# Weight conversion on VectorE in five pieces, and an opening in another order, in a spectral mixer with an MLP

## The chip, the cores and the metric

One NeuronCore of a Trainium2 chip runs the whole kernel in one launch. The metric is device microseconds of one execution; lower is better.

## The reference

For each of 8 batches, x (3072 positions, 256 channels) goes through a real FFT over the positions, a complex 256x256 product with bias, soft shrinkage and the inverse FFT; the result feeds an MLP with a softplus.

```python
X = np.fft.rfft(x, axis=1)                       # x: 8 x 3072 x 256
Yr = Xr @ w_r - Xi @ w_i + b_r
Yi = Xr @ w_i + Xi @ w_r + b_i
Y = sign(Y) * max(abs(Y) - 0.01, 0)              # Yr and Yi apart
y = np.fft.irfft(Y, n=3072, axis=1)              # then 24576 x 256
h = y @ w_in                                     # 256 x 2048
g = np.maximum(h, 0) + np.log1p(np.exp(-np.abs(h)))
out = g @ w_out                                  # 2048 x 256
```

## The kernel before, in words

Both FFTs are matmuls with constant tables. One batch passes through the stages `s1` (16 products of 96x512, the first DFT factor), `s3` (the second factor, for 12 groups `gp`), `mix` (complex weights and bias; the shrinkage `cl`, `shrunk`, `sh`, `sl` follows), `s4` (first inverse factor) and `s5` (second inverse factor). Between s1 and s3 (`a_dr`, from batch 1 on) and between s4 and s5 (`d_dr`) the data go through DRAM. The MLP takes y in products that save a multiplication by Strassen-like sums: its first layer writes `psc` and `pse`, VectorE adds (`t`, L542), ScalarE makes the softplus, `gh` and VectorE `gl` (L558), the high and low halves of the second layer's operand `pso`. Each fp32 product is three fp32r products of a high and a low half (L213 to L215).

The MLP's weights arrive as float64 words and are turned on the chip into a high and a low half, eight times `w1` (7 tiles of 128x128 with the Strassen sums, 896 KB with both halves) and eight times `w2` (512 KB). `load_w` brings the words, `split_w` converts: VectorE makes the exponent and mantissa by bit operations (L158 to L164), GpSimd multiplies and adds (L171, L180 to L184), VectorE makes the four sums (L188 to L191), ScalarE copies the high half (L192), VectorE subtracts (L196) and `store` writes the tile to DRAM (L99). The converted tile is tagged `wp` and there is one buffer for it (`bufs=1`). `stream_w` (L209) later loads a converted weight for every key of four MLP steps.

The order is written out by a table of steps (L674 to L760): 72 steps −72 to −1 in front, which take batch 0 through all stages and batch 1 through s1 (the first key's y comes from four `s5` at −4 to −1), then 768 MLP steps, four per key. In each step the program issues the MLP's products, one product of the other stages (`steps`), the loads that `fill` has for it, and what an earlier step has put into the queue `later`. Ten conversions begin in front, one every fourth step from −46; six begin at MLP steps 1, 5, 9, 13, 17 and 21. SyncE's queue (SP) carries nearly every DMA in program order; a wait of one holds the ones behind it. DMAs signal on eight hardware lanes in turn (DMAHW0 to 7). While `early` holds (up to step −2), tiles come from other tags and s1's odd columns are copied from PSUM by VectorE (L265).

Of the kernel before, what the change touches and what calls it, by code (L numbers as in the profile page):

```python
# [17 lines left out]
P = 128  # L18
# [15 lines left out]
def tile_spectral_mixer_mlp(ctx, tc, x, w_r, w_i, bias, bias_0, w_in, w_out, f, f_hi, f_lo, g1, g3, g3_hi, g3_lo, hm, out):  # L34
# [101 lines left out]
    def load_w(which, m2):  # L136

        if early:
            st = sb.tile([P, 1024 + 4 * N1], F32, tag="dp", name="w64", bufs=4)[:, :1024]
        else:  # L140
            st = sb.tile([P, 1024], F32, tag="w64", name="w64", bufs=1)
        nc.sync.dma_start(st.rearrange("p (a n) -> p a n", a=2).bitcast(U32), (w_in if which else w_out)[:, m2])
        stages[which, m2] = st

    def split_w(which, m2):

        st = stages.pop((which, m2)).bitcast(U32).rearrange("p (n w) -> p n w", w=2)
# [12 lines left out]
        v.tensor_scalar(out=ui, in0=ti, scalar1=0xFF800000, scalar2=None, op0=ALU.bitwise_and)  # L164

        def second():
            nc.scalar.mul(lw.bitcast(F32), lw, 2.0 ** -52)
            later.append(third)

        def third():  # L170
            g.tensor_tensor(out=u, in0=lw.bitcast(F32), in1=u, op=ALU.mult)  # L171
            n = 7 * P if which else 2 * D
            w = sb.tile([P, 2 * 7 * P], F32R, tag="wp", name="wp", bufs=1)[:, :2 * n]
            hi, lo, src = w[:, :n], w[:, n:], w[:, n:].bitcast(F32)
            if which:

                tm, um = [a.rearrange("p (k m n) -> p m k n", k=2, m=2) for a in (t, u)]
                a21 = tm[:, 1, 0]
                o = [src[:, i * P:(i + 1) * P] for i in range(7)]
                g.tensor_tensor(out=src[:, A11 * P:(A11 + 2) * P].rearrange("p (k n) -> p k n", k=2), in0=tm[:, 0], in1=um[:, 0], op=ALU.add)  # L180
                g.tensor_tensor(out=a21, in0=a21, in1=um[:, 1, 0], op=ALU.add)
                g.tensor_tensor(out=o[A22], in0=tm[:, 1, 1], in1=um[:, 1, 1], op=ALU.add)
            else:
                g.tensor_tensor(out=src, in0=t, in1=u, op=ALU.add)  # L184

            def high():
                if which:
                    v.tensor_tensor(out=o[S1], in0=a21, in1=o[A22], op=ALU.add)  # L188
                    v.tensor_tensor(out=o[S3], in0=o[A11], in1=a21, op=ALU.subtract)
                    v.tensor_tensor(out=o[S2], in0=o[S1], in1=o[A11], op=ALU.subtract)  # L190
                    v.tensor_tensor(out=o[S4], in0=o[A12], in1=o[S2], op=ALU.subtract)  # L191
                nc.scalar.copy(hi, src)  # L192
                later.append(low)

            def low():
                v.tensor_tensor(out=lo, in0=src, in1=hi.bitcast(F32), op=ALU.subtract)  # L196
                store((w1_dr if which else w2_dr)[m2][:, :], w.bitcast(F32), ("w", which, m2))

            later.append(high)

        later.append(second)
# [46 lines left out]
    def s1(b, c):  # L248
# [141 lines left out]
    def mix_sums(b, gp, lh, ll, real):  # L390
# [20 lines left out]
        v.tensor_scalar(out=cl, in0=z, scalar1=-LAM, scalar2=LAM, op0=ALU.max, op1=ALU.min)  # L411

        t = sb.tile([P, 512], F32, tag="v", name="shrunk", bufs=1)
        for c in range(2):
            for g in range(2):
                src = slice(g * 64, g * 64 + 64), slice(c * D, c * D + D)
                dst = slice(c * 64, c * 64 + 64), slice(g * D, g * D + D)
                v.tensor_tensor(out=t[dst], in0=z[src], in1=cl[src], op=ALU.subtract)
# [213 lines left out]
    with tc.manual_schedule():  # L632
# [71 lines left out]
        for t, i, j in ((t0 + 15, 0, 4), (t0 + 16, 4, 12), (t0 + 22, 12, NG)):  # L704
            at(t, nc.sync.dma_start, g1_0[:, i:j], g1[:, i:j])
        at(t0 + 18, nc.sync.dma_start, bias0, bias_0)
        at(-6, nc.sync.dma_start, bias_sb, bias)
        for k in range(2):
            at(t0 + 14 + k, load_mix, k)
            at(t0 + 18 + k, split_mix, k)  # L710
        for j in range(NM):
            t = t0 + 26 + 4 * j if j < 10 else 1 + 4 * (j - 10)
            at(t - (6 if j < 10 else 2), load_w, (j + 1) % 2, j // 2)
            before[t] = (j + 1) % 2, j // 2
        for c in need_d(0):
            at(first.index(("s4", 0, NP - 1)) + t0 + 4, load_d, 0, 0, c)
        for i, (t, src) in enumerate(((fh, f_hi), (fl, f_lo), (g3h, g3_hi), (g3l, g3_lo))):
            at(4 * i - 9, nc.gpsimd.dma_start, t, src)
        at(-1, early.clear)
        for k in range(2):  # L720
            at(-1, load_mix, k)
            at(1 + 2 * k, combine_mix, 1 + k)

        nt = NT
        for b in range(B):
            for bp in range(1, NPAIR):
                plan_s5(b, bp, nt * b + 2 * NM * bp - 14)
            if b + 1 < B:
                plan_mix(b + 1, *((5, 4.9) if b == 0 else (nt * b - 4, 5.6)))
                plan_s5(b + 1, 0, nt * (b + 1) - 14)  # L730
        for b in range(2, B):
            plan_s1(b, *((14, 4.6) if b == 2 else (nt * (b - 2) - 4, 5.4)))
        keys = [(b, bp, mp) for b in range(B) for bp in range(NPAIR) for mp in range(NM // 2)]
        for i, key in enumerate(keys):
# [3 lines left out]
            else:  # L738
                at(-3, stream_w, 1, 0, key)
                at(-2, stream_w, 0, 0, key)  # L740
        keys.append(None)
        for i in range(min([*fill, *steps]), nt * B + 3):
            due = len(later)
            other = split_w(*before.pop(i)) if i in before else iter(())
            if i >= 0:
                g, s = divmod(i, 4)
# [11 lines left out]
            for _ in other:  # L758
                pass
# [101 lines left out]
```

## Time and profile before

| | us |
|---|---|
| median of three runs (2713.51 to 2718.43) | 2714.6 |
| the profiled execution | 2714.95 |
| its span, first to last instruction | 2713.2 |
| TensorE (PE) busy | 2614.4 (96%) |
| VectorE (DVE) busy | 1624.9 (60%) |
| ScalarE (ACT) busy | 1708.0 (63%) |
| GpSimd (POOL) busy | 302.0 (11%) |

All rows are from the one profiled execution. The shares are means over a span that is mostly the steady MLP; the steps in front and the first MLP steps have to be read in stretches of their own. In a row of waits, "a <- b" is an engine that stood idle before instruction a until b ended. SPq is the queue of SyncE's DMAs.

### The profile page before, as it was taken

The numbers are of one execution on the slowest core, as the hardware profiler recorded it, in microseconds if no ns is written. First come the engines' busy times: TensorE is split into PE (matmuls) and PEld (weight loads), VectorE is DVE, ScalarE is ACT, GpSimd is POOL, SyncE is SP. The second block draws the span as 40 slices with busy tenths as digits, with TensorE's granted clock in tenths as the row PEclk, the third lists the DMA queues.
The fourth block names the chain that finished last, engine by engine and source line by source line (L and its number), as shares of the span: only waits on it lengthen the run. The fifth ranks groups of instructions, "written<-read, shape, count | busy, mean of one in ns | idle before, by whom it ended". The sixth has DMA issues, their size and how long they took to land.

```text
span 2713.2 us, 36252 instructions
## 1 busy us (share of the span) xinstructions
PE 2614.4 (96%) x13053; PEld 2190.6 (81%) x13053; DVE 1624.9 (60%) x2701; ACT 1708.0 (63%) x3093; POOL 302.0 (11%) x302
## 2 busy tenths in 40 slices
PE   7658999999999999999999999999999999999999
PEld 5437888888888888888878888788887888888887
DVE  3647665567656666466664666556664666644554
ACT  2336666666666666666666666666666666666665
POOL 1422110100101101011011010110010000000000
PEclk8869999999999999999999999999999999999999
DMA  5656556565565564555645655556555455455543
GB/s 195 206 191 222 181 167 199 172 197 166 167 197 171 185 189 143 192 183 177 202 145 174 205 176 161 186 164 198 174 173 177 162 169 188 142 160 176 176 154 111
DMA packets 186115, 479.73 MB, mean 177 GB/s; under 512 B 18096, under 2 KB 86960, under 8 KB 185936
## 3 DMA queue, kind: packets, MB, share of 16 engines
q1 hardware_dynamic: 185376, 476.95, 54.9%
q8 instruction: 103, 1.69, 0.3%
q0 software_dynamic: 560, 0.47, 0.1%
q14 instruction: 76, 0.62, 0.1%
HBM read 390.31 MB, written 83.89 MB: 175 GB/s over the span
## 4 chain that ended last, share of the span: by engine, by line
PE 87%; DMA 5%; DVE 4%; ACT 2%; POOL 1%; issue 1%; SPq 0%; DVEq 0%; ACTq 0%; POOLq 0%
PE pso L213 12%; PE pso L214 12%; PE pso L215 12%; PE psc L213 6%; PE psc L215 6%; PE psc L214 6%; PE pse L213 5%; PE pse L215 5%; PE pse L214 5%; PE psf L460 4%; PE psf L214 4%; PE psf L215 4%; PE psf L213 4%; PE psf L292 2%; DMA a_dr<-a 2%
## 5 line engine op out<-in xcount | busy, mean ns | idle before, releaser
L558 DVE TENSOR_TENSOR gl<-t,gh 128x512 fp32r<-128x512 f32 x768 | 532.3, 693 | 367.0 <-ACT gh L552 363.7
L542 DVE TENSOR_TENSOR t<-pse,t 128x512 f32<-128x512 f32 x576 | 396.2, 688 | 441.5 <-ACT t L537 285.1
L537 ACT COPY t<-psc 128x512 f32<-128x512 f32 x576 | 336.9, 585 | 492.3 <-PE psc L215 490.4
L213 PE MATMUL pso<-gh,w 128*128 128x512 f32 x1536 | 616.5, 401 | 0.0
L214 PE MATMUL pso<-gl,w 128*128 128x512 f32 x1536 | 600.6, 391 | 0.0
L215 PE MATMUL pso<-gh,w 128*128 128x512 f32 x1536 | 600.2, 391 | 0.0
L552 ACT CAST gh<-t 128x512 fp32r<-128x512 f32 x768 | 476.8, 621 | 61.8 <-PE pso L215 38.1
L548 ACT ACTIVATE t<-t 128x512 f32<-128x512 f32 x576 | 364.4, 633 | 68.7 <-DVE t L542 67.9
L215 PEld LDWEIGHTS pso<-gh,w 128*128 128x128 f32 x1536 | 289.1, 188 | 62.5
L213 PE MATMUL psc<-y_sb,w 128*128 128x512 f32 x768 | 302.8, 394 | 34.8 <-ACT t L537 16.8
L213 PEld LDWEIGHTS pso<-gh,w 128*128 128x128 f32 x1536 | 290.2, 189 | 54.7
L214 PEld LDWEIGHTS pso<-gl,w 128*128 128x128 f32 x1536 | 290.2, 189 | 51.4
L215 PE MATMUL psc<-y_sb,w 128*128 128x512 f32 x768 | 300.5, 391 | 0.0
L214 PE MATMUL psc<-y_sb,w 128*128 128x512 f32 x768 | 300.1, 391 | 0.0
L213 PE MATMUL pse<-y_sb,w 128*128 128x512 f32 x576 | 228.2, 396 | 14.7 <-DVE t L542 14.6
L114 POOL TENSOR_TENSOR xl<-xt,xh 96x512 fp32r<-96x512 f32 x96 | 124.5, 1300 | 960.7 <-ACT xh L105 823.7
L215 PE MATMUL pse<-y_sb,w 128*128 128x512 f32 x576 | 225.4, 391 | 0.0
L214 PE MATMUL pse<-y_sb,w 128*128 128x512 f32 x576 | 225.3, 391 | 0.0
L494 POOL TENSOR_TENSOR y_sb<-raw,y_sb 128x512 fp32r<-128x512 f32 x72 | 95.8, 1331 | 1130.8 <-ACT y_sb L491 1130.8
L213 PEld LDWEIGHTS psc<-y_sb,w 128*128 128x128 f32 x768 | 144.8, 189 | 72.3 <-ACT t L537 22.3
L215 PEld LDWEIGHTS psc<-y_sb,w 128*128 128x128 f32 x768 | 144.9, 189 | 31.1
L214 PEld LDWEIGHTS psc<-y_sb,w 128*128 128x128 f32 x768 | 144.9, 189 | 29.6
(123 smaller groups left out, 3640.8 us busy)
## 6 DMA issues: line engine op xcount, KB each, us to landing
w<-w_dr SPq DMA_DIRECT2D x192, 896.0 KB
w<-w_dr SPq DMA_DIRECT2D x192, 512.0 KB
dp<-d_dr SPq DMA_DIRECT2D x80, 384.0 KB
xt<-in_x SPq DMA_DIRECT2D x128, 192.0 KB
d_dr<-d SPq DMA_DIRECT2D x96, 256.0 KB
out_y<-ot SPq DMA_DIRECT2D x96, 256.0 KB
ap<-a_dr SPq DMA_DIRECT2D x84, 256.0 KB
a_dr<-a SPq DMA_DIRECT2D x96, 192.0 KB
```

The costliest lines, as they stand in the source:

```text
L114: (eng or nc.vector).tensor_tensor(out=lo, in0=src, in1=hi.bitcast(F32), op=ALU.subtract)
L213: nc.tensor.matmul(ps, wh, xh, start=start, stop=False, skip_group_check=more)
L214: nc.tensor.matmul(ps, wh, xl, start=False, stop=False, skip_group_check=more)
L215: nc.tensor.matmul(ps, wl, xh, start=False, stop=stop, skip_group_check=more)
L292: nc.tensor.matmul(xv[:, g, k], t[:, g, k * P:(k + 1) * P], g1_t[:, g].rearrange("p (c s) -> p c s", c=2), start=True, stop=True,)
L460: nc.tensor.matmul(ps[:, t - blk * BLK:t - blk * BLK + n], d_sb[b, blk // 2, n2 // 4][0][:, n2 % 4, k * P:(k + 1) * P], d_sb[b, blk // 2, ...
L494: eng.tensor_tensor(out=lo, in0=raw[j], in1=hi.bitcast(F32), op=ALU.subtract)
L537: nc.scalar.copy(t, banks[bank])
L542: nc.vector.tensor_tensor(out=t, in0=banks[bank], in1=t, op=ALU.add)
L548: nc.scalar.activation(t, banks[bank] if bank else t, AF.Softplus)
L552: nc.scalar.copy(gh, ct[key, what])
L558: nc.vector.tensor_tensor(out=gl, in0=ct.pop((key, what)), in1=gh.bitcast(F32), op=ALU.subtract)
```

## The change

Conversions. `split_w` runs all its arithmetic on VectorE (ScalarE keeps the square, the scaling and the high half), in five pieces, one in each of five steps; the store is issued one step after the fifth. Eight begin in front (steps −56, −52, then every seventh from −47 to −12), eight at MLP steps 0, 3, 6, ... 21. The `wp` tile is taken in piece three. It still has one buffer.

Opening. The tables `g1_0`, `bias0` and the mixing weights of the front are loaded by GpSimd's queue, and earlier; x is loaded 6 steps ahead; s1's PSUM copies are all ScalarE's; the first key's `w2` and `w1` are loaded at steps −16 and −14 instead of −2 and −3, the first `dp` tiles two steps earlier; the lows of `T1`, `T2`, `T4` are VectorE's in front.

Steady part. The tile `a` (s1's output on its way to `a_dr`, L264) has the pool's two buffers instead of one. The shrinkage behind `mix` begins one step later, its high half two, and the low half with it. Batch 1's `mix` steps begin at step 9 instead of 5, batch 2's `s1` at step 8 instead of 14.

```diff
 def load_mix(c):
-    nc.sync.dma_start(...)
+    (nc.gpsimd if early else nc.sync).dma_start(...)
 def load_w(which, m2):
-    if early:
+    if m2 < 6:                                   # words in the tag dp, else w64
 def split_w(which, m2):                          # the old one is printed above
     nc.scalar.activation(u, hw.bitcast(F32), AF.Square)
     v.tensor_scalar(out=ti, in0=hw, scalar1=3, scalar2=0x3FFFFFF8, ...)
     v.scalar_tensor_tensor(out=ti, in0=hw, scalar=0xC0000000, in1=ti, ...)
+    nc.scalar.mul(lw.bitcast(F32), lw, 2.0 ** -52)
     yield
     v.scalar_tensor_tensor(out=t, in0=u, scalar=2.0 ** -30, in1=t, ...)
+    v.tensor_scalar(out=ui, in0=ti, scalar1=0xFF800000, ...)
+    v.tensor_tensor(out=u, in0=lw.bitcast(F32), in1=u, op=ALU.mult)
     yield
+    w = sb.tile([P, 2 * 7 * P], F32R, tag="wp", name="wp", bufs=1)[:, :2 * n]
+    if which:
+        v.tensor_tensor(out=src[:, A11 * P:(A11 + 2) * P]..., in0=tm[:, 0], in1=um[:, 0], op=ALU.add)
+        v.tensor_tensor(out=a21, in0=a21, in1=um[:, 1, 0], op=ALU.add)
+        v.tensor_tensor(out=o[A22], in0=tm[:, 1, 1], in1=um[:, 1, 1], op=ALU.add)
+        ...                                      # S1 to S4 as before
+    else:
+        v.tensor_tensor(out=src, in0=t, in1=u, op=ALU.add)
+    yield
+    nc.scalar.copy(hi, src)
+    yield
+    v.tensor_tensor(out=lo, in0=src, in1=hi.bitcast(F32), op=ALU.subtract)
+    store((w1_dr if which else w2_dr)[m2][:, :], w.bitcast(F32), ("w", which, m2))
 def s1(b, c):
-            a = sb.tile([P, 512], F32, tag="a", name="a", bufs=1)[:N1]
-    (nc.vector.tensor_copy if early and c % 2 else nc.scalar.copy)(a, ps[:N1, :])
+            a = sb.tile([P, 512], F32, tag="a", name="a")[:N1]
+    nc.scalar.copy(a, ps[:N1, :])
 def mix_sums(b, gp, lh, ll, real):
     v.tensor_tensor(out=z, in0=ps, in1=z, op=ALU.add)
+    def shrink():                                # cl, shrunk, then split into sh, sl
+        ...
+    later.append(shrink)
 # the planner
-    at(max(t0 - 1, t - (11 if b == 0 else 5 if i < 4 else 7)), load_x, b, i)
+    at(max(t0 - 1, t - 6), load_x, b, i)
+    for k in range(2):
+        at(t0 + 4 + k, load_mix, k)
-    for t, i, j in ((t0 + 15, 0, 4), (t0 + 16, 4, 12), (t0 + 22, 12, NG)):
-        at(t, nc.sync.dma_start, g1_0[:, i:j], g1[:, i:j])
-    at(t0 + 18, nc.sync.dma_start, bias0, bias_0)
+    for t, i, j in ((t0 + 6, 0, 4), (t0 + 12, 4, 12), (t0 + 20, 12, NG)):
+        at(t, nc.gpsimd.dma_start, g1_0[:, i:j], g1[:, i:j])
+    at(t0 + 8, nc.gpsimd.dma_start, bias0, bias_0)
     for j in range(NM):
-        t = t0 + 26 + 4 * j if j < 10 else 1 + 4 * (j - 10)
-        at(t - (6 if j < 10 else 2), load_w, (j + 1) % 2, j // 2)
-        before[t] = (j + 1) % 2, j // 2
+        t = t0 + 16 + 4 * j if j < 2 else t0 + 25 + 7 * (j - 2) if j < 8 else 3 * (j - 8)
+        at(t - (6 if t < 0 else 3 if j < 12 else 2), load_w, (j + 1) % 2, j // 2)
+        before.setdefault(t, []).append(split_w((j + 1) % 2, j // 2))
-        at(first.index(("s4", 0, NP - 1)) + t0 + 4, load_d, 0, 0, c)
+        at(last + 2, load_d, 0, 0, c)            # last: the step of s4(0, 11), -14
-            plan_mix(b + 1, *((5, 4.9) if b == 0 else (nt * b - 4, 5.6)))
+            plan_mix(b + 1, *((9, 4.9) if b == 0 else (nt * b - 4, 5.6)))
-        plan_s1(b, *((14, 4.6) if b == 2 else (nt * (b - 2) - 4, 5.4)))
+        plan_s1(b, *((8, 4.5) if b == 2 else (nt * (b - 2) - 4, 5.4)))
-            at(-3, stream_w, 1, 0, key)
-            at(-2, stream_w, 0, 0, key)
+            at(last, stream_w, 1, 0, key)
+            at(last - 2, stream_w, 0, 0, key)
+    ...                                          # each step runs one piece of every open conversion
```

Two places in the order of the instructions. The first is the engine that writes a new `wp` tile, around the ninth and tenth conversions. Before, it is GpSimd: L180 and L184 are the first to write the tiles wp_1017 and wp_1063, and what stands behind them are GpSimd's own few instructions (L494 is a low half of y, L753 a constant's load).

```order
L180 TENSOR_TENSOR wp_1017<-wt_995,wu_996 128x256 [waits DMAHW2_49,Pool_49]
L181 TENSOR_TENSOR wt_995<-wt_995,wu_996 128x128
L182 TENSOR_TENSOR wp_1017<-wt_995,wu_996 128x128
L753 DMA fh_72<-in_f_hi 96x96
L171 TENSOR_TENSOR wu_1045<-w64_975,wu_1045 128x512 [waits DMAHW3_49,DVE_49,Activation_49]
L184 TENSOR_TENSOR wp_1063<-wt_1044,wu_1045 128x512 [waits DMAHW6_49,Pool_49]
L753 DMA fl_73<-in_f_lo 96x96
L494 TENSOR_TENSOR y_sb_1089<-raw_1092,y_sb_1089 128x512 [waits DVE_49,Activation_49]
```

After the change the same place is on VectorE (L186 is the subtraction that ends tile wp_1146, L182 the first writer of the next tile, wp_1229; L532 and L548 are the MLP's `t` and `gl`).

```order
L164 TENSOR_TENSOR wu_1161<-w64_1118,wu_1161 128x512 [waits DVE_49]
L186 TENSOR_TENSOR wp_1146<-wp_1146 128x896
L548 TENSOR_TENSOR gl_1212<-t_1176,gh_1178 128x512 [waits DMAHW3_49,Activation_49]
L532 TENSOR_TENSOR t_1207<-pse_1203,t_1207 128x512 [waits PE_49,Activation_49]
L548 TENSOR_TENSOR gl_1215<-t_1135,gh_1210 128x512 [waits Activation_49]
L131 SCALAR_TENSOR_TENSOR wsum_1217<-stage_1140,stage_1142 128x512 [waits DMAHW2_49,DMAHW1_49]
L182 TENSOR_TENSOR wp_1229<-wt_1160,wu_1161 128x512 [waits DMAHW2_49,DVE_49]
L548 TENSOR_TENSOR gl_1243<-t_1207,gh_1239 128x512 [waits Activation_49]
```

The wait for the lane of the previous tile's store moved from GpSimd to VectorE, with the MLP's `t` and `gl` in front of it and behind it.

The second place is SP's queue at the first weights that the MLP needs. Before, they are the last of these rows (w1_1107 and w2_1124), behind the stores of batch 1's s1 (a_dr), the bias and the store of a converted weight.

```order
L753 DMA bias_sb_76<-in_bias 128x512 [waits DMAHW1_49]
L99 DMA a_dr_199<-y1_80 4x24x512 [waits DMAHW2_49,DVE_49]
L99 DMA a_dr_199<-y1_80 4x24x512 [waits DMAHW3_49,Activation_49]
L99 DMA w2_dr4_93<-wp_1063 128x1024 [waits DMAHW4_49,DVE_49]
L99 DMA a_dr_199<-y1_80 4x24x512 [waits DMAHW5_49,DVE_49]
L209 DMA w1_1107<-w1_dr0_81 128x1792 [waits DMAHW6_49]
L209 DMA w2_1124<-w2_dr0_89 128x1024 [waits DMAHW7_49]
```

After the change (L195 is the same load, L222 a load of x):

```order
L195 DMA w2_960<-w2_dr0_89 128x1024 [waits DMAHW2_49]
L222 DMA xt_966<-in_x 96x512 [waits DMAHW3_49,PE_49]
L99 DMA d_dr_393<-d_956 128x2x256 [waits DMAHW4_49,Activation_49]
L222 DMA xt_974<-in_x 96x512 [waits DMAHW5_49,PE_49]
L195 DMA w1_976<-w1_dr0_81 128x1792 [waits DMAHW6_49,Pool_49]
L99 DMA a_dr_205<-y1_80 4x24x512 [waits DMAHW7_49,Activation_49]
L99 DMA w1_dr3_84<-wp_946 128x1792 [waits DMAHW0_49,DVE_49]
```

Both loads moved in front of the last stores of `d_dr` and of the loads of `dp`.

## Rows read from the trace of the kernel before

**Rows 1.** The stretches of the span: from:to, length, then busy us (and count) of each engine, the granted clock of TensorE, the DMA engines' share and GB/s. 27.58 is the first s3, 128.06 the end of the last s4 of batch 0, 147.49 the first s5, 174.02 the first MLP product.

```profile
0.00:27.58 27.58, 19.63 (x41) 7.21 (x41) 8.16 (x12) 8.23 (x13) 0.92 (x5) 0.97 0.65 204
27.58:96.27 68.69, 56.40 (x346) 50.47 (x347) 38.67 (x71) 20.45 (x41) 25.99 (x31) 0.86 0.59 195
96.27:128.06 31.79, 16.90 (x73) 11.50 (x72) 17.80 (x34) 10.29 (x19) 12.28 (x12) 0.79 0.66 212
128.06:147.49 19.43, 10.85 (x19) 3.18 (x18) 9.45 (x18) 5.83 (x10) 4.86 (x7) 0.68 0.69 199
147.49:174.02 26.53, 10.42 (x48) 10.31 (x49) 7.00 (x10) 6.00 (x11) 6.84 (x8) 0.50 0.70 229
174.02:284.04 110.02, 94.48 (x441) 75.74 (x442) 81.38 (x133) 67.51 (x122) 31.23 (x33) 0.93 0.56 194
...
360.00:2713.00 2353.00, 2332.15 (x11725) 1970.57 (x11723) 1414.53 (x2342) 1541.96 (x2789) 210.63 (x202) 1.00 0.54 173
```

**Rows 2.** What PE waited for, by the instruction that waited and what ended the wait: us in all, times, longest; from 30 to 75 (first row), 75 to 125 (the next two) and 125 to 175 (the last three).

```profile
PE psf L215 <- DVE w L114: 7.4, 3, 3.8
...
PE psf L432 <- POOL z L387: 4.1, 2, 2.6
PE psf L215 <- DVE w L114: 4.0, 2, 3.1
...
PE psc L213 <- DMA w<-w_dr: 16.1, 1, 16.1
PE psf L432 <- POOL z L387: 9.0, 1, 9.0
PE psf L460 <- DMA dp<-d_dr: 5.9, 1, 5.9
```

**Rows 3.** Pieces of the chain that ended last, from 100 to 174 us: start, us, what.

```profile
100.86 0.70 DVE wt L160
101.65 0.70 DVE wt L162
102.38 0.43 DVE wu L164
...
124.68 1.26 POOL z L387
...
146.06 10.38 DMA w_dr<-wp
...
161.16 12.72 DMA w<-w_dr
```

**Rows 4.** VectorE's groups from 128 to 300 us: line, operation, out<-in, shapes, count | busy us, mean ns | idle before.

```profile
L558 DVE TENSOR_TENSOR gl<-t,gh 128x512 fp32r<-128x512 f32 x29 | 23.3, 803 | 16.6 <-ACT gh L552 16.6
...
L160 DVE SCALAR_TENSOR_TENSOR wt<-w,wt 128x512 uint32<-128x512 uint32 x8 | 6.5, 813 | 0.3
L162 DVE SCALAR_TENSOR_TENSOR wt<-wu,wt 128x512 f32<-128x512 f32 x8 | 6.4, 800 | 0.8
...
L158 DVE TENSOR_SCALAR wt<-w 128x512 uint32<-128x512 uint32 x8 | 4.5, 558 | 0.0
L196 DVE TENSOR_TENSOR wp<-wp 128x896 fp32r<-128x896 f32 x4 | 4.3, 1087 | 1.2 <-ACT wp L192 1.1
...
L196 DVE TENSOR_TENSOR wp<-wp 128x512 fp32r<-128x512 f32 x5 | 3.4, 688 | 15.8 <-ACT wp L192 15.7
...
L191 DVE TENSOR_TENSOR wp<-wp 128x128 f32<-128x128 f32 x4 | 1.2, 292 | 0.1
```

**Rows 5.** What VectorE waited for from 174 to 284 us: us in all, times, longest.

```profile
DVE gl L558 <- ACT gh L552: 16.1, 13, 2.4
DVE t L542 <- PE pse L215: 11.4, 4, 8.0
```

**Rows 6.** Three stores of a converted weight as SP issues them (start us, us, w1 at 60.51 and 146.06, w2 at 132.67), with the store of `a_dr` that held SP, and GpSimd's first write of the next tile behind each (start, us, idle before and what ended it).

```profile
60.51 0.34 SPq L99 DMA_DIRECT2D w_dr<-wp  x1
66.35 1.29 POOL L184 TENSOR_TENSOR wp<-wt,wu 128x512 f32<-128x512 f32 x1 [1.03 <-DMA w_dr<-wp]
...
132.67 0.42 SPq L99 DMA_DIRECT2D w_dr<-wp  x1
139.14 0.72 POOL L180 TENSOR_TENSOR wp<-wt,wu 128x256 f32<-128x256 f32 x1 [5.50 <-DMA w_dr<-wp]
...
146.06 0.51 SPq L99 DMA_DIRECT2D w_dr<-wp  x1
156.58 1.26 POOL L184 TENSOR_TENSOR wp<-wt,wu 128x512 f32<-128x512 f32 x1 [8.87 <-DMA w_dr<-wp]
...
150.50 9.08 SPq L99 DMA_DIRECT2D a_dr<-y  x2
```

**Rows 7.** Waits of ScalarE and of PE from 360 us to the end (us in all, times, longest), and one stretch of 10 us behind such a wait, columns as in rows 1.

```profile
ACT a L265 <- DMA a_dr<-a: 25.1, 7, 4.3
...
PE psc L213 <- ACT t L537: 11.4, 6, 2.8
...
1390.00:1400.00 10.00, 7.20 (x34) 6.26 (x33) 3.71 (x7) 5.05 (x9) 1.26 (x1) 0.83 0.14 47
```

**Rows 8.** One low half `sl` as VectorE writes it, and its use by PE in s4.

```profile
1060.81 0.68 DVE L114 TENSOR_TENSOR sl<-shrunk,sh 128x512 fp32r<-128x512 f32 x1
...
1065.14 0.39 PE L214 MATMUL psf<-sl,g3h 128*128 128x512 f32 x1
```

More of the change, by code (lines that the diff above doesn't have):

```diff
@@ L155, in split_w @@
         ti, ui = t.bitcast(U32), u.bitcast(U32)
-        v, g = nc.vector, nc.gpsimd
+        v = nc.vector
         nc.scalar.activation(u, hw.bitcast(F32), AF.Square)
         v.tensor_scalar(out=ti, in0=hw, scalar1=3, scalar2=0x3FFFFFF8, op0=ALU.logical_shift_left, op1=ALU.bitwise_and)
-        yield
         v.scalar_tensor_tensor(out=ti, in0=hw, scalar=0xC0000000, in1=ti, op0=ALU.bitwise_and, op1=ALU.bitwise_or)
+        nc.scalar.mul(lw.bitcast(F32), lw, 2.0 ** -52)
         yield
         v.scalar_tensor_tensor(out=t, in0=u, scalar=2.0 ** -30, in1=t, op0=ALU.is_ge, op1=ALU.mult)
+        v.tensor_scalar(out=ui, in0=ti, scalar1=0xFF800000, scalar2=None, op0=ALU.bitwise_and)
@@ L163, in split_w @@
+        v.tensor_tensor(out=u, in0=lw.bitcast(F32), in1=u, op=ALU.mult)
         yield
[L164 to L199, printed above, removed]
@@ L410, in mix_sums @@
         v.tensor_tensor(out=z, in0=ps, in1=z, op=ALU.add)
[L411 to L418, printed above, removed]
         sh = sb.tile([P, 512], F32R, tag="sh", name="sh", bufs=1)
         sl = sb.tile([P, 512], F32R, tag="sl", name="sl", bufs=1)
-        later.append(lambda: split(t, sh, sl, None, ("s", b, gp)))
+        def shrink():
+            v.tensor_scalar(out=cl, in0=z, scalar1=-LAM, scalar2=LAM, op0=ALU.max, op1=ALU.min)
+            t = sb.tile([P, 512], F32, tag="v", name="shrunk", bufs=1)
+            for c in range(2):
+                for g in range(2):
+                    src = slice(g * 64, g * 64 + 64), slice(c * D, c * D + D)
+                    dst = slice(c * 64, c * 64 + 64), slice(g * D, g * D + D)
+                    v.tensor_tensor(out=t[dst], in0=z[src], in1=cl[src], op=ALU.subtract)
+            later.append(lambda: split(t, sh, sl, None, ("s", b, gp)))
+        later.append(shrink)
         s_t[b, gp] = sh, sl
@@ L510, in b12 @@
         keep(key, 1, ps)
-        put_split(key, T1, 0, nc.gpsimd)
+        put_split(key, T1, 0, nc.vector if early else nc.gpsimd)
     def b22(key, ps):
@@ L664, in plan_s5 @@
         def plan_s5(b, bp, start):
+            if (b, bp) == (1, 0):
+                start += 2
             for c in need_d(bp):
@@ L743, in tile_spectral_mixer_mlp, with prepare @@
             due = len(later)
-            other = split_w(*before.pop(i)) if i in before else iter(())
+            parts = before.pop(i, [])
+            def prepare():
+                for part in parts:
+                    if next(part, part) is None:
+                        before.setdefault(i + 1, []).append(part)
             if i >= 0:
+                prepare()
                 g, s = divmod(i, 4)
@@ L757, in tile_spectral_mixer_mlp @@
                 slot_second(s, key, prev)
-            for _ in other:
-                pass
+            else:
+                prepare()
         assert not fill and not steps and not before
```

27 lines of the change are left out of this document (18 added, 9 removed).

## The prediction

> **What bounds the kernel now.** I read the stretches first, because the page's shares mix a steady MLP with a front that is nothing like it. [rows 1] give, for each stretch, its length and then the busy time of PE, PEld, DVE, ACT and POOL. From 360 us to the end PE is busy 2332.15 of 2353.00 at clock 1.00: only PE's own work or its few gaps count there. In front it is different. From 27.58 (the first s3) to 174.02 (the first MLP product) 146.4 us pass, and PE is busy 56.40 + 16.90 + 10.85 + 10.42 = 94.6 of them. From 174.02 to 284.04 (MLP steps 0 to 28, while the last conversions run) 110.02 pass with 94.48 of PE and 81.38 of DVE. So some 52 us of PE's idle time lie before the first MLP product, some 15 in the first 28 steps, 21 behind 360.
>
> Then the waits of PE name what ended each gap. [rows 2]: in the loop of s3, mix and s4 it is VectorE's low half `w` (7.4 and 4.0 us) and GpSimd's `z` (4.1); behind the loop one `z` (9.0), the load of `dp` (5.9) and the first weight of the MLP (16.1). Then the chain of waits shows why these came late. [rows 3]: the chain runs through conversion work on VectorE (0.70, 0.70 and 0.43 of one conversion) before it reaches a `z` at 124.68, and the first weight's load, 12.72 us long, is issued only at 161.16, behind a converted weight's store that took 10.38 from 146.06. The reader is to see that the opening is bound by order and by queues, not by an engine's total.
>
> **Part A, the opening (to the first MLP product).**
> The loop from 27.58 to 96.27 has 68.69 − 56.40 = 12.3 us without PE. The conversions now come every seventh step, their sums no longer hold GpSimd in front of `z`, and `w` and `z` find a free engine. A conversion costs VectorE more: L158 and L164 0.43 each, L160 and L162 0.70 each [rows 3], a product 0.69 like any 512 columns [rows 4], and for w1 adds of 256 and twice 128 columns (0.4 + 2 × 0.29), four sums (4 × 0.29) and the low half (1.09, all in [rows 4]): 6.2 us; for w2 2.95 + 0.69 + 0.69 = 4.3. Before it was 4.5 and 2.9. Six conversions of 5.2 us on average are left behind 27.58, 31 us where there were eight of 3.7, 30 us: VectorE, busy 38.67 + 17.80 = 56.5 of 100.5 us up to 128.06 [rows 1], will be busy about 58 of 74, so it still has room. I take −12.
> From 96.27 to the end of s4(0, 11) at 128.06 PE is idle 14.9 of 31.79, 9.0 of it for one `z` behind a conversion. I take −14.
> From there to the first s5 (147.49) the way is d's store, its landing, the load of `dp`. The loads are issued two steps sooner, but 1.4 MB of weights now stand in front of them: −2, between −6 and +5.
> The s5 products last 10.42 at clock 0.50, the 1.2 GHz level [rows 1]: unchanged.
> The wait of 16.1 for the first weight goes: it is issued at s4(0, 11), some 28 us before its use, and needs 12.72. What is late next is `dp`, so nothing follows. −16.1.
> The ramp up to 27.58 I cost at nothing: constants leave SP's queue, which is behind x there, and go to GpSimd's, where they take the same DMA engines as x does. ScalarE takes s1's odd copies over from VectorE; ACT is busy 8.23 of 27.58, which hides them.
> A = −12 − 14 − 2 − 16.1 = **−44**, between −33 (half of the loop's and z's waits stay) and −52 (ramp and dp gain as well).
>
> **Part B, MLP steps 0 to 28.** VectorE's demand: 81.4 before. Eight conversions instead of six: 4 × 6.2 + 4 × 4.3 = 42.0 against 3 × 4.5 + 3 × 2.9 = 22.2, so +19.8. One mix step of batch 1 less (start 9 for 5): four operations of 512 columns, `cl` 0.43 and six of 256 at about 0.42, −5.7. Beside GpSimd's conversion work VectorE's operations were stretched: the means in [rows 4] are 813, 800 and 558 ns for L160, L162 and L158 against 700, 700 and 430, and 803 for L558 against 690; that is 8 × 0.34 + 29 × 0.11 = 6 us, which goes, since GpSimd has none of it left. Together 89.5 us.
> Then the wait that moves. There is one `wp` buffer, conversions come every three steps, the store leaves one step after piece five and piece three of the next needs the buffer in that same step. So VectorE itself must wait for the landing of the store, with every `t` and `gl` of the MLP behind it in its queue, and PE behind those. This happens seven times (four stores of w1, three of w2). How long a store takes: in [rows 6] GpSimd's first write of the next tile starts when it has landed; w1 60.51 to 66.35, 5.8 us, and 146.06 to 156.58, 10.5 us; w2 132.67 to 139.14, 6.5 us. Before, these waits cost GpSimd only. With 8.2 and 6.5, 4 × 8.2 + 3 × 6.5 = 52 us; between the end of the low half and the waiting instruction VectorE has some three operations of 0.69, 2 us each time, so 52 − 14 = 38. Its idle time of now, 28.6 us (16.1 for `gh`, 11.4 for `pse` [rows 5]), mostly falls into these waits; I keep 10. 89.5 + 38 + 10 = 137.5, against 110: B = **+28**. Bounds: with every store at 5.8 and the 3.3 us of a whole step in front of it (2353 us over some 720 steps) it is 7 × 2.5 = 18 and +8; with all at 10.5, nothing in front and no other idle time, 73 and +52.
> The Trainium skill, page "DMA: Bandwidth & Descriptors", section "Anatomy of one DMA", gives about 2.0 us plus the bytes over 436 GB/s for a DMA of GpSimd's queue, that is an estimate of 4.1 us for w1 and 3.2 for w2, by which the waits would be 26 − 14 = 12 us and the total 2656. These stores are SP's, and the trace has 5.8 to 10.5 and 6.5 with other loads around, so the rows decide.
>
> **Part C, the steady part.** ScalarE waits 25.1 us in 7 places behind 360 for the single tile `a` to be stored, and PE then waits 11.4 in 6 for ScalarE's `t` [rows 7]. After such a gap the granted clock falls: it is 0.83 over the 10 us from 1390, part of them at 1.2 instead of 2.4 GHz, which loses 1.7 us. I take this for five of the eight places (one lies before 360), an estimate of 8.5. With two tiles both go: 11.4 + 8.5 = −20. The shrinkage's step later costs something: `sl` is written at 1060.81 to 1061.5 and read at 1065.14 [rows 8], 3.6 us later; a step is 3.3 us, so 0.3 is left. A good part of the 84 uses will have no slack: bounds 0 and 84 × 0.1; I take +3. It gives ScalarE and VectorE room in return, which costs nothing where PE bounds. C = **−17**, between −20 and −10.
>
> **Sum.** 2714.95 − 44 + 28 − 17 = **2682**. The profiled execution is 0.35 above the median of the three runs, which is nothing here.
>
> **The rivals.**
> Rival 1, the stores hide. SP issues each at once, they land in 5.8 us and a step's own work stands in front; what VectorE waits, PE's queue of finished `psc` and `gh` absorbs. For it: VectorE has 110 − 89.5 = 20 us of slack. Against it: 10.5 us was also seen, with eight loads of `dp` in front of one store. With no wait left the stretch is VectorE's 89.5 and 10 idle, or PE's 94.5 with half of its 15 us of gaps, 102, so B = −8; with waits of 13 us it is +3. The time is 2646 to 2657, say **2650**. Chance 0.22.
> Rival 2, slower than before: VectorE behind the one `wp` buffer costs more than the opening gains. SP holds things long (a store of `a_dr` before the weights held it 9.08 us [rows 6]); if each of the seven stores leaves 5 us late, waits are 38 + 35 = 73, and after each PE restarts at the lower clock, 7 × 1.7 = 12: B = 89.5 + 73 + 10 + 12 − 110 = +74 and the time **2728**. It decides from B = +66, waits of 11 us each. Against it: only one store in [rows 6] took that long. Chance 0.11.
> Rival 3, the opening becomes bound by transfers. 195 GB/s × 68.69 + 212 × 31.79 = 20.1 MB were moved from 27.58 to 128.06 [rows 1]; two conversions (2.4 MB) move out; 17.7 MB in 74 us are 239 GB/s, where the busiest stretch has 229. At 205 GB/s it takes 86 us, and `dp`, behind the two weights, comes 7 later: A = −25, the time **2701**. The Trainium skill, "SBUF — State Buffer", section "SBUF: two separate sides", speaks against the constants' new queue: a DMA of GpSimd's queue can be starved while VectorE runs certain operations. No run so far shows it; by that rule the first tables would come late as well, by an operation of VectorE each. Chance 0.13.
> Rival 4, two tiles `a` do not close the gaps, because the store itself comes late from SP's queue: C = +3, the time **2702**. Chance 0.06.
>
> **How the numbers follow.** The forecast, 2682, has 0.48; its own range is 2664 to 2702. Rival 1 adds the low end, 2648; rivals 3 and 4 lie inside; the high end of 2712 leaves rival 2 and some bad sums out. A measurement of this kernel can tell about 0.2%, 5.4 us. Faster (below 2709): 0.46 + 0.22 + 0.11 + 0.05 = 0.84; within 0.2%: 0.05; slower (above 2720): 0.11.
>
> **What would show it.** The first MLP product at about 130 instead of 174.02; no PE wait for a weight there. In the 28 steps behind it, VectorE idle some 48 us, ended by stores of converted weights (L174, L182), the stretch about 138 us long, with a lower granted clock. Behind it no ScalarE wait for `a`, and small PE waits for `sl`. It is wrong if VectorE's waits for stores are below 18 or above 73 us, if the first product comes after 142, or if `a`'s gaps are still there.

## The result, and the profile after

2741.7 us (median of 4 runs, 2740.05 to 2742.89) against 2716.5 before (median of 4, 2713.51 to 2723.62): the ratio is 1.0088, interval [1.0067, 1.011]. The change makes the kernel **slower** by 0.9%, where 2682 was forecast. The profiled execution took 2742.89, its span is 2740.4 (before 2713.2).

The stretches of the changed kernel that answer to [rows 1], same columns: to the first s3, to the last s3, to the last s4 of batch 0, to the first s5, to the first MLP product; then from the first `gl` to the 29th, and from the 65th to the last.

```profile
0.00:34.80 34.80, 26.60 (x40) 7.92 (x41) 4.77 (x10) 15.03 (x25) 4.47 (x11) 0.90 0.77 224
34.80:99.33 64.53, 50.29 (x346) 45.59 (x347) 46.99 (x89) 23.03 (x45) 14.80 (x15) 0.89 0.53 181
99.33:113.28 13.95, 12.91 (x72) 9.04 (x71) 13.38 (x24) 5.35 (x10) 5.26 (x6) 1.00 0.81 258
113.28:140.82 27.54, 11.43 (x19) 3.14 (x18) 5.67 (x10) 7.30 (x13) 0.55 (x1) 0.74 0.75 243
140.82:150.92 10.10, 10.10 (x49) 10.09 (x48) 3.73 (x6) 4.02 (x7) 0.00 (x0) 0.50 0.61 210
162.10:307.10 145.00, 109.62 (x464) 85.87 (x463) 92.56 (x172) 74.90 (x135) 15.17 (x19) 0.86 0.52 169
440.10:2732.00 2291.90, 2268.44 (x11359) 1903.52 (x11358) 1347.48 (x2266) 1502.80 (x2701) 198.32 (x194) 1.00 0.54 172
```

PE's waits in it, as in [rows 2]: from 0 to 150 (first two), from 162 to 308 (next three), from 330 to the end (last two).

```profile
PE psf L240 <- DMA xt<-in_x: 20.4, 7, 7.1
PE psf L201 <- DVE w L114: 11.2, 2, 10.4
...
PE pse L199 <- DVE t L532: 26.3, 11, 7.2
PE psc L199 <- ACT t L527: 6.8, 4, 3.4
PE psf L200 <- DVE sl L114: 1.5, 1, 1.5
...
PE pse L199 <- DVE t L532: 17.7, 27, 1.6
PE psf L200 <- DVE sl L114: 5.9, 13, 0.5
```

The times of VectorE's 768 `gl`, one for each MLP step, divide the span without gaps (read from both timelines):

| | before | after | difference | forecast |
|---|---|---|---|---|
| start to first MLP product | 174.0 | 150.9 | −23.1 | A: −44 |
| start to first `gl` | 179.1 | 162.1 | −17.0 | |
| first to 29th `gl` | 115.9 | 145.0 | +29.1 | B: +28 |
| 29th to 65th | 135.0 | 133.0 | −2.0 | |
| 65th to last | 2274.8 | 2292.0 | +17.2 | C: −17 |

The reader is to see that B came out as forecast, that A gave less than half, and that the steady part, the one that was to gain, lost 17. The waits for the store stood on VectorE as said: seven from 162 to 308, 36.7 us (38 in the sum), three behind stores of w2 (L174) and four behind stores of w1 (L182). One of them, as SP issues the store, as VectorE waits behind its `ll` of 201.35, and as PE waits for `t`:

```profile
DVE wp L174 <- DMA w_dr<-wp: 20.9, 3, 8.3
DVE wp L182 <- DMA w_dr<-wp: 15.8, 4, 7.2
...
201.01 0.37 SPq L99 DMA_DIRECT2D w_dr<-wp  x1
...
207.14 0.69 DVE L182 TENSOR_TENSOR wp<-wt,wu 128x512 f32<-128x512 f32 x1 [5.37 <-DMA w_dr<-wp]
...
209.09 0.79 PE L199 MATMUL pse<-y_sb,w 128*128 128x512 f32 x1 [4.59 <-DVE t L532]
```

### The profile page after: what moved, and what is told of

Its sections match the earlier page's. It is cut to its first block, busy times and chain, and to the rows that moved or that the text cites. A ratio compares the mean times of both kernels' runs of the same rounds, so it can differ in the third digit from the quotient of the medians.

```text
span 2740.4 us, 36219 instructions
## 1 busy us (share of the span) xinstructions
PE 2630.9 (96%) x13053; PEld 2182.1 (80%) x13053; DVE 1607.9 (59%) x2736; ACT 1728.2 (63%) x3109; POOL 253.9 (9%) x257
## 4 chain that ended last, share of the span: by engine, by line
PE 87%; DVE 6%; DMA 5%; ACT 1%; issue 1%; SPq 0%; POOL 0%; DVEq 0%; ACTq 0%
PE pso L199 12%; PE pso L200 12%; PE pso L201 12%; PE psc L199 6%; PE psc L201 6%; PE psc L200 6%; PE pse L199 5%; PE pse L201 4%; PE pse L200 4%; PE psf L450 4%; PE psf L200 4%; PE psf L201 4%; PE psf L199 4%; PE psf L278 3%; DMA w_dr<-wp 2%; DVE shrunk L408 1%
## 5 line engine op out<-in xcount | busy, mean ns | idle before, releaser
L548 DVE TENSOR_TENSOR gl<-t,gh 128x512 fp32r<-128x512 f32 x768 | 530.0, 690 | 301.6 <-ACT gh L542 297.5
L532 DVE TENSOR_TENSOR t<-pse,t 128x512 f32<-128x512 f32 x576 | 396.4, 688 | 505.6 <-ACT t L527 325.4
L199 PE MATMUL psc<-y_sb,w 128*128 128x512 f32 x768 | 302.3, 394 | 12.5 <-ACT t L527 11.6
L199 PE MATMUL pse<-y_sb,w 128*128 128x512 f32 x576 | 233.2, 405 | 44.4 <-DVE t L532 44.0
L200 PE MATMUL pse<-y_sb,w 128*128 128x512 f32 x576 | 226.5, 393 | 0.1
L201 PE MATMUL pse<-y_sb,w 128*128 128x512 f32 x576 | 226.4, 393 | 0.0
L199 PEld LDWEIGHTS psc<-y_sb,w 128*128 128x128 f32 x768 | 145.2, 189 | 48.2 <-ACT t L527 15.8
L199 PEld LDWEIGHTS pse<-y_sb,w 128*128 128x128 f32 x576 | 108.7, 189 | 90.8 <-DVE t L532 69.2
L201 PEld LDWEIGHTS psc<-y_sb,w 128*128 128x128 f32 x768 | 144.7, 188 | 31.1
```

The source lines that it names most:

```text
L199: nc.tensor.matmul(ps, wh, xh, start=start, stop=False, skip_group_check=more)
L200: nc.tensor.matmul(ps, wh, xl, start=False, stop=False, skip_group_check=more)
L201: nc.tensor.matmul(ps, wl, xh, start=False, stop=stop, skip_group_check=more)
L532: nc.vector.tensor_tensor(out=t, in0=banks[bank], in1=t, op=ALU.add)
L548: nc.vector.tensor_tensor(out=gl, in0=ct.pop((key, what)), in1=gh.bitcast(F32), op=ALU.subtract)
```

## The experiments

Times are medians; "before" beside them is the kernel before on the same chip. "Steady" is from the 65th `gl` to the last, the "stretch" from the first to the 29th. These, and the rows, are from one profiled execution of each kernel. Steady repeats well: it is 2291.9 to 2292.9 in the six kernels with the changed shrinkage untouched. The opening repeats less well: in the four kernels whose opening is that of the change (the changed one and the three that edit only its shrinkage) the first MLP product comes between 148.7 and 151.7 and the first `gl` between 160.4 and 163.6, so a shift of these two by some 3 us shows nothing.

**The steady part.** Two tiles `a` alone, in the kernel before:

```diff
-                a = sb.tile([P, 512], F32, tag="a", name="a", bufs=1)[:N1]
+                a = sb.tile([P, 512], F32, tag="a", name="a")[:N1]
```

> The kernel before with two buffers for the tile a and nothing else. Theory G: the gaps at the store of a (ScalarE 25.1 us in 7 places, PE 11.4 us in 6 behind 360 us) and the clock lost behind them were a real cost: 2695-2705, no ScalarE wait for a_dr. Rival R: the gap only moves to the next thing that needs the late store or VectorE; 2711-2717, another wait of PE of about 2 us in the same places.

2691.1 against 2716.7, ratio 0.9912 [0.9893, 0.9931]. ScalarE no longer waits for `a_dr`, steady is 2257.7 against 2274.8, and 6.6 us more are gained before it. Theory G holds; the gain, 24 to 26 us, is larger than the 20 of the sum.

The changed kernel with the shrinkage put back:

```diff
-        def shrink():
-            ...
-        later.append(shrink)
+        v.tensor_scalar(out=cl, in0=z, ...)      # and the four subtractions, in the step of mix
+        later.append(lambda: split(t, sh, sl, None, ("s", b, gp)))
```

> The changed kernel with the shrinkage as before (cl and shrunk in the step of mix, high half one step later). Theory S: in the steady part the later shrinkage makes PE wait for VectorE's t (27 times, 17.7 us from 330 us on) and for sl (13 times, 5.9 us), each with a restart of about 0.27 us; with the old place these go and the two tiles a are left as a gain: 2741.7 falls to 2715-2725, PE's waits behind 330 us fall from 24 to under 5 us. Rival A: the second tile a, or the extra DMA traffic, makes those waits; the time stays within 2737-2745 and the waits for t stay.

2708.9 against 2716.7, ratio 0.997 [0.9959, 0.9981]: 33 us below the changed kernel, by more than theory S said. First `gl` and stretch stay (163.6, 145.1); steady is 2259.2, as with two tiles alone. The steady stretch of the changed kernel stands above; here are this kernel's and PE's waits in it from 330 us on:

```profile
440.10:2699.00 2258.90, 2255.45 (x11361) 1907.82 (x11360) 1368.53 (x2265) 1494.42 (x2701) 200.35 (x194) 1.00 0.54 175
...
PE pse L199 <- DVE t L528: 3.2, 12, 0.3
PE psc L199 <- ACT lh L292: 0.4, 2, 0.3
```

PE's idle time there is 3.5 us against 23.5, which is 20 of the 33. The other 13 are in PE's busy time, 2255.45 against 2268.44 for the same matmuls (11361 and 11359): the first matmul behind a wait takes 0.50 us instead of 0.39 (the last row of the next fence) and the one behind it follows later, and there are 27 more such waits, which is part of it; the rest the rows don't show.

Where the burst (`cl` and the four subtractions `shrunk`) stands on VectorE, first in the changed kernel, with the product that waits for it, then with the old place, at the same step of batch 2:

```profile
868.49 0.69 DVE L114 TENSOR_TENSOR ll<-psf,lh 128x512 fp32r<-128x512 f32 x1 [1.85 <-ACT lh L292]
869.10 0.41 DVE L327 TENSOR_TENSOR sum<-psf,sum 128x256 f32<-128x256 f32 x1
869.42 0.42 DVE L402 TENSOR_SCALAR cl<-z 128x512 f32<-128x512 f32 x1
869.88 1.72 DVE L408 TENSOR_TENSOR shrunk<-z,cl 64x256 f32<-64x256 f32 x4
871.62 0.69 DVE L569 COPY ot<-pso 128x512 f32<-128x512 f32 x1
872.35 0.69 DVE L532 TENSOR_TENSOR t<-pse,t 128x512 f32<-128x512 f32 x1
...
873.09 0.50 PE L199 MATMUL pse<-y_sb,w 128*128 128x512 f32 x1 [0.85 <-DVE t L532]
```

```profile
860.69 0.43 DVE L397 TENSOR_SCALAR cl<-z 128x512 f32<-128x512 f32 x1
861.15 1.72 DVE L404 TENSOR_TENSOR shrunk<-z,cl 64x256 f32<-64x256 f32 x4
862.90 0.69 DVE L544 TENSOR_TENSOR gl<-t,gh 128x512 fp32r<-128x512 f32 x1
863.51 0.68 DVE L114 TENSOR_TENSOR ll<-psf,lh 128x512 fp32r<-128x512 f32 x1
864.11 0.41 DVE L327 TENSOR_TENSOR sum<-psf,sum 128x256 f32<-128x256 f32 x1
864.44 0.68 DVE L565 COPY ot<-pso 128x512 f32<-128x512 f32 x1
865.08 0.69 DVE L528 TENSOR_TENSOR t<-pse,t 128x512 f32<-128x512 f32 x1
```

With the old place the 2.1 us are over before `ll`; one step later VectorE idles 1.85 us in front of `ll` and the burst stands between `sum` and `ot`, `t`. PE waits for that `t` until 873.09, 0.85 us. The two things that were moved, apart: the burst as before, only the high and the low half as late as changed.

```diff
-        later.append(lambda: split(t, sh, sl, None, ("s", b, gp)))
+        later.append(lambda: later.append(lambda: split(t, sh, sl, None, ("s", b, gp))))
```

> The changed kernel with cl and the four subtractions back in the step of mix, but the high and the low half as late as changed (two and three steps behind mix). Theory B (place of the burst): what costs is that cl and the subtractions (2.1 us of VectorE) stand one step later in front of ot and t; PE's waits for t behind 330 us fall from 17.7 to under 5 us, those for sl stay at 4 to 8, the time is 2713-2722. Theory L (lateness of the halves): the waits for t stay above 12 us and the time above 2733.

2713.0 against 2715.5, ratio 0.9998 [0.9985, 1.001]. Its steady stretch, and PE's waits from 330 us on:

```profile
430.90:2696.30 2265.40, 2259.05 (x11361) 1905.61 (x11360) 1366.95 (x2266) 1495.23 (x2701) 199.45 (x194) 1.00 0.55 174
...
PE psf L200 <- DVE sl L114: 3.8, 8, 0.5
PE pse L199 <- DVE t L528: 3.2, 11, 0.4
```

So of the 32.8 us that steady lost to the shrinkage, the place of the burst is 26.6 and the lateness of the halves 6.2. Theory B. The medians of the three kernels (2741.7, 2713.0, 2708.9) divide the loss into 28.7 and 4.1.

The reverse, the burst late and the high half in its own step:

```diff
-            later.append(lambda: split(t, sh, sl, None, ("s", b, gp)))
+            split(t, sh, sl, None, ("s", b, gp))
```

> The changed kernel with cl and shrunk one step later as changed, but the high half in that same step and the low half one step behind it, so that sl is ready as many steps before s4 as it was before the change. Theory B (burst): cl and the four subtractions now stand in a step where VectorE has ot and t to do, and PE waits for t; the waits for t behind 330 us stay at 15 to 20 us, those for sl (5.9) go, the time falls to 2731-2738. Theory L (lateness of sl alone): both go and the time falls to 2710-2718.

2868.8, ratio 1.0579 [1.0552, 1.0605]: neither theory. PE's waits for `t` of VectorE are 3.3 us here, for `sl` none; but ScalarE's copy `sh` now stands directly behind the subtractions, in front of the softplus, and waits for them, 81 times from 330 us on, and PE waits 103.0 us for ScalarE's `t`:

```profile
ACT sh L105 <- DVE shrunk L408: 221.7, 81, 3.5
...
PE psc L199 <- ACT t L527: 59.3, 43, 2.4
PE psc L199 <- ACT t L538: 43.7, 27, 2.3
```

It shows what a step between an operation and its user on another engine is worth here, and doesn't tell the two theories apart.

**The first 28 steps.** The changed kernel with the conversions at the steps of before, all on VectorE still:

```diff
-            t = t0 + 16 + 4 * j if j < 2 else t0 + 25 + 7 * (j - 2) if j < 8 else 3 * (j - 8)
+            t = t0 + 26 + 4 * j if j < 10 else 1 + 4 * (j - 10)
```

> The changed kernel with the conversions begun at the steps of the kernel before (ten in front from -46 every fourth step, six at MLP steps 1, 5, ... 21), still all on VectorE in five pieces. Theory W: what costs in MLP steps 0 to 28 is VectorE's wait for the previous tile's store; with four steps between conversions and two fewer of them the waits fall from 38 to under 20 us, and the stretch from the first gl to the 29th from 145 to 115-125 us; in front VectorE waits for more stores, +5 to +15 on the first product; the time is 2722-2735. Rival V: VectorE's added work itself is the cost; the stretch stays over 130 us.

2715.9 against 2716.7, ratio 1.0001 [0.9988, 1.0014]: 26 us below the changed kernel and below the 2722 of the expectation. The first product comes at 162.0, the first `gl` at 173.5 (+11.4), and the stretch is 108.4 against 145.0 and, with GpSimd's help, 115.9 before. Its row, VectorE's two store waits in it, and (last two rows) those in front, from 0 to 162:

```profile
173.50:281.90 108.40, 97.50 (x463) 79.22 (x463) 86.32 (x154) 71.45 (x130) 16.94 (x19) 0.94 0.62 208
...
DVE wp L182 <- DMA w_dr<-wp: 0.7, 1, 0.7
DVE wp L174 <- DMA w_dr<-wp: 0.4, 1, 0.4
...
DVE wp L182 <- DMA w_dr<-wp: 16.7, 5, 11.1
DVE wp L174 <- DMA w_dr<-wp: 9.9, 2, 9.6
```

Theory W: with six conversions four steps apart the one buffer is free in time in the MLP, and VectorE does all their arithmetic without loss; the run doesn't part the two, fewer conversions and more steps between them. Two conversions fewer are 6 us of VectorE's busy time (92.56 against 86.32), the rest of the 36.6 is waiting. In front the same four steps do not free the buffer: VectorE waits 26.6 us for stores there, in seven places. With the old shrinkage as well:

> The changed kernel with the shrinkage and the conversions' steps as before; conversions still all on VectorE, opening and two tiles a as changed. If the two losses are separate (33 us for the shrinkage, 26 for the table), the time is 2741.7 - 33 - 26 = 2680 to 2686. If VectorE in MLP steps 0 to 28 is what both share, the sum is smaller: 2690 to 2700.

The edits are those of the old shrinkage and of the conversions' old steps. 2681.9 against 2713.0, ratio 0.9892 [0.9874, 0.991]. Steady is 2258.0 and the stretch 106.4, each as with its own edit alone: the losses are separate.

**The opening.** Four edits of the changed kernel, one of the kernel before. The front's tables back on SP's queue:

```diff
-        (nc.gpsimd if early else nc.sync).dma_start(st...)       # w_r, w_i; g1_0 and bias0 likewise
+        nc.sync.dma_start(st...)                                 # at the old steps, split_mix two steps later
```

> The changed kernel with the front's tables g1_0, bias0 and the mixing weights on SP's queue at their old steps. Theory Q: GpSimd's queue starts 2.3 MB at once beside x, which makes x and so the first s3 late (34.80 against 27.58 before); the first s3 comes at 27 to 30 and the first MLP product 5 to 8 us before 150.9. Rival N: the queue does not matter, x of 20 steps is bound by its own transfers or by the words of the first two conversions; the first s3 stays at 33 to 36.

2741.5. The first s3 comes at 29.9 instead of 34.8 (34.2 to 34.8 in the four with the same opening), as theory Q said, but the first product at 148.9 and the first `gl` at 160.8, only 2.0 and 1.3 sooner, which is within the spread. The run moves the queue and the steps of the loads together and doesn't tell them apart.

The front conversions six steps apart:

```diff
+            t = t0 + 16 + 6 * j if j < 8 else 3 * (j - 8)
```

> The changed kernel with the eight front conversions every sixth step from -56 (the second came four steps behind the first). Theory F: VectorE's wait of 12.5 us for the first store, and PE's 10.4 us for w behind it, come from those four steps; VectorE's waits there fall below 5 us in all, PE's wait is gone and the first MLP product comes at 140 to 146. Rival L: the time comes back as later waits for x, dp or z; the first product stays at 148 to 152.

2742.8. PE's wait for `w` falls from 11.2 to 3.5 us, VectorE still waits 10.5 for one store, and `z` (6.9) takes the place: first product 153.5, 1.5 later than rival L said. So the four steps are not what makes that store late. The rows of the changed kernel show where it stands: the first tile is finished at 37.97, but SP issues its store only at 47.89, behind six other DMAs.

```profile
36.88 1.09 DVE L186 TENSOR_TENSOR wp<-wp 128x896 fp32r<-128x896 f32 x1
...
38.52 1.48 SPq L99 DMA_DIRECT2D a_dr<-y  x1
...
43.83 3.97 SPq L264 DMA_DIRECT2D ap<-a  x2
47.89 2.41 SPq L99 DMA_DIRECT2D w_dr<-wp  x1
...
58.28 0.69 DVE L182 TENSOR_TENSOR wp<-wt,wu 128x512 f32<-128x512 f32 x1 [12.54 <-DMA w_dr<-wp]
...
60.76 0.58 PE L201 MATMUL psf<-wmh,w 128*128 128x256 f32 x1 [10.40 <-DVE w L114]
```

With six steps the tile is finished at 38.10 and its store issued at 49.44. No run moves this store in SP's queue.

x as early as before:

```diff
-                at(max(t0 - 1, t - 6), load_x, b, i)
+                at(max(t0 - 1, t - (11 if b == 0 else 5 if i < 4 else 7)), load_x, b, i)
```

> The changed kernel with x loaded as early as before (11 steps for batch 0, 5 or 7 for batch 1). Theory X: the waits of PE for x in the opening (20.4 us in 7 places) come from the shorter lead; they fall under 8 us and the first MLP product comes at 138-143 instead of 150.9, the time is 2729-2735. Rival D: the transfers as such are too many there (front constants, 1.4 MB of weights before dp); the waits move to dp or ap, and the first product stays at 147-155.

2740.5. PE's waits for x fall to 11.6, the first s3 starts at 30.6 (34.8), the first s5 at 131.4 (140.8) and the first product at 142.2 (150.9): theory X as far as the first product. But the first `gl` comes at 160.7, 1.4 sooner, and the time is not that of theory X: VectorE's first conversion instruction of the MLP waits 4.41 us for its words, until 156.54, with `t` behind it, and PE waits 6.86 for ScalarE behind that. The words loaded at step −14 instead of −3, with x early:

```diff
-            at(t - (6 if t < 0 else 3 if j < 12 else 2), load_w, (j + 1) % 2, j // 2)
+            at(t - (14 if j == 8 else 6 if t < 0 else 3 if j < 12 else 2), load_w, (j + 1) % 2, j // 2)
```

> The changed kernel with x as early as before and the words of the conversion at MLP step 0 loaded at step -14 instead of -3. Theory K: with x early the first MLP product came at 142.2, but the first gl only at 160.7 against 162.1, since VectorE's first conversion instruction (L158) waited until 156.5 for its words (issued at 143.3, behind the stores of a_dr) with the MLP's first t behind it; now L158 does not wait, the first gl comes at 150 to 154 and the time is 2731 to 2735. Rival M: another thing (y of the first s5, the first weights, ScalarE) holds the first gl at 157 or later and the time stays at 2738-2742.

2740.1. The wait for the words is gone, yet the first `gl` comes at 159.6: rival M. The first s5 starts at 134.8, the first product at 146.3, and then PE waits for y's high half, which ScalarE and VectorE make behind s5:

```profile
153.36 0.80 PE L199 MATMUL pse<-y_sb,w 128*128 128x512 f32 x1 [5.42 <-ACT y_sb L469]
157.13 0.80 PE L199 MATMUL psc<-y_sb,w 128*128 128x512 f32 x1 [1.63 <-ACT t L527]
```

The same question in the kernel before, with two tiles `a`:

```diff
-                at(-3, stream_w, 1, 0, key)
-                at(-2, stream_w, 0, 0, key)
+                at(first.index(("s4", 0, NP - 1)) + t0, stream_w, 1, 0, key)
+                at(first.index(("s4", 0, NP - 1)) + t0 - 2, stream_w, 0, 0, key)
```

> The kernel before with two tiles a and the first key's weights loaded at steps -16 and -14 (w2, w1) instead of -2 and -3. Theory E: PE's wait of 14.2 us for the first weight goes and nothing takes its place: 2691 falls to 2676-2680, the first product comes 12 to 15 us sooner. Rival P: 1.4 MB in front of d_dr and dp on SP's queue make dp late by as much; the first s5 comes 8 to 12 us later and the time is 2686-2692.

2689.7 against 2713.0, ratio 0.9925 [0.9908, 0.9943], beside 2691.1 without the edit. The first product comes 12.7 us sooner (171.8 to 159.1), as theory E said, s5 is not later (147.2, 147.4), so rival P's reason is wrong, though the time is in its range; but the first `gl` gains only 5.0, and the times of the two kernels can't be told apart (the other's ratio is 0.9912 [0.9893, 0.9931]):

```profile
147.37 10.42 PE L460 MATMUL psf<-dp 96*128 96x96 f32 x48 [4.25 <-DMA dp<-d_dr]
159.08 0.80 PE L213 MATMUL psc<-y_sb,w 128*128 128x512 f32 x1 [1.29 <-ACT y_sb L479]
...
166.57 0.80 PE L213 MATMUL pse<-y_sb,w 128*128 128x512 f32 x1 [5.32 <-ACT y_sb L479]
```

Behind the wait for the weight stood the making of y, hidden by it.

Some smaller moves of the change were in every run of the changed kernel, and no run takes them apart: batch 1's first s5 two steps later, four constants six steps later, the MLP's mixing tables two to three steps later, and a conversion's piece in front of the step's products in the MLP instead of behind them.

**A version that beats both.** The changed kernel with the old shrinkage, early x and words, and the conversions so:

```diff
+            t = t0 + 16 + 5 * j if j < 10 else 4 * (j - 10)
```

> The changed kernel with the old shrinkage, ten conversions in front every fifth step from -56 and six at MLP steps 0, 4, ... 20, x as early as before, the words of the conversion at step 0 loaded at -13. Theory: no store wait in MLP steps 0 to 28 (stretch 108 us, first gl to 29th), front waits smaller than with every fourth step: first gl at 155 to 165, the time 2660 to 2672. Rival: the front with ten conversions on VectorE is bound by VectorE and the stores as in the run with the old table (first gl 173 to 176): 2678 to 2684.

2676.0 against 2713.2, ratio 0.9872 [0.9844, 0.99]. The stretch is 105.0. The first `gl` comes at 167.5 and the time is 4 us above the forecast's range; VectorE waits 30.8 us for stores in front, as the rival said. Against the old shrinkage and the old steps together (2681.9, ratio 0.9892) the gain is within the intervals.

## Why the prediction was wrong, point by point

2741.7 is 60 us above 2682: 34 of them are C (+17.2 for −17), 21 A (−23.1 for −44) and 6 more come between the first product and the first `gl`; B is 1 off. With the shrinkage put back, everything else as changed, the time was 2708.9.

**C is the step that failed**, and in it "I take +3" for the shrinkage one step later. It measured +33 (2741.7 to 2708.9; steady 2292.0 against 2259.2). I priced it by the slack between `sl` and its use alone [rows 8]; that part is real, about 6 us. The other 26.6 I put at less than nothing: "It gives ScalarE and VectorE room in return". `cl` and the four subtractions are 2.1 us of VectorE that move as well, and I asked neither what stands behind them on VectorE in the new step (`ot` and `t`) nor who waits for that `t`: PE, 27 times and 17.7 us from 330 us on, against 12 times and 3.2 with the old place. The two tiles `a` were right in mechanism and worth 24 to 26, not 20.

**A** failed too, outside its own range: −44 forecast, −23.1 measured at the first product and −17.0 at the first `gl`. By its own steps: the ramp, costed at nothing, took 7.2 longer; 4.9 of these come back with the tables on SP's queue at their old steps, 4.2 with early x alone. The loop to the last s3 gained 4.2, not 12: VectorE waited 12.5 us for a front store, which SP issued 10 us after its tile was finished, and PE 10.4 behind it; I had put the store waits into the MLP only. The stretch to the last s4 gained 17.8, where 14 was taken. From there to s5 it lost 8.1, where −2 was taken, by x's shorter lead: with early x the first s5 comes at 131.4. The wait for the weight went as said (26.5 to 10.1 us from s5 to the first product), but "nothing follows" was wrong: y's halves follow. From the first s5 to the first `gl` 31.6 us became 21.3. Three edits, each meant to take one of these waits away, moved the first product by between +2.6 and −8.7 us and the first `gl` by +3.0 to −1.4; only the −8.7 is clear of the spread. This reads as several chains that hold the opening at once; which one ends last at the first `gl` when all are eased is not settled here.

Rival 3 had −25 for A, near the −23.1, but its reason is not in the rows: it took 205 GB/s as what the transfers can do, and from the last s3 to the first s5 258 and 243 were moved, while the loop, which gained least, moved 181. Nor can VectorE have made GpSimd's tables late: its first instruction starts at 29.86, and the last table took 13.5 us from its issue at 5.00.

**B** was right in mechanism and, in part by luck, in size: +29.1 against +28, store waits of 36.7 against 38, VectorE busy 92.6 against 89.5. The two prices of a store were wrong in opposite directions: 8.2 was taken for w1 and 6.5 for w2, and from SP's issue to VectorE's first write behind it the four w1 took 4.2 to 8.6 (mean 5.9), the three w2 6.0 to 9.5 (mean 8.1). The 0.43 of L158 stands in no row of [rows 3]; it was 0.41 to 0.44 in the changed kernel from 162 to 308.

The Trainium skill's estimate for a DMA of GpSimd's queue ("DMA: Bandwidth & Descriptors", section "Anatomy of one DMA") was below the rows of these stores of SP's, 4.1 for w1 and 3.2 for w2; the w1 store issued at 201.01, for one, held VectorE until 207.14, 6.1 us. Rival 2, the one that ended slower, had the wrong place, VectorE behind `wp` at 11 us each; they were 5.2 each. The total was slower because of the shrinkage, for which no rival stood.

## What to carry to other kernels

A step that moves work is priced on the engine's order, not on the slack of its result: write down what stands behind the moved instructions in the new place, and who waits for that. A single buffer whose writer changes engine moves its wait too, to everything in the new engine's queue; six conversions four MLP steps apart instead of eight three apart took the waits from 36.7 us to 1.1. The count of steps alone is no rule: four steps in front left 26.6 us, and there the store's place in SP's queue has to be read as well. And a wait at the end of a chain is worth only what the next chain leaves of it: here 5 of 14 us at the first `gl`.

## What the runs showed that was not expected

PE's busy time, as the profile counts it, is not constant for the same matmuls: with 27 more short waits in the steady part, idle time is 20 us more and busy time 13. Of the granted clock the rows show 0.86 in the stretch with the seven store waits and 0.94 in that with two short ones (both a mix of 1.2 and 2.4 GHz), and 0.50, the 1.2 GHz level, for s5 in both kernels.
